# Reordering the loads of a planned attention and expert kernel: first v loads after the first q cast, batch 1 v blocks between casts, batch 2 loads after batch 1 v, dearer v loads in the planner's model

## The chip, the cores and the metric

The kernel runs on one core of one Trainium2 chip. The metric is the device time of one execution in microseconds; lower is better. The kernel before took 360.42 us (median of three, 358.01 to 360.87). A profiled execution has a "span" from its first to its last instruction, some 2 us less than its device time. Each execution has a state: "slow" where it is over 1.5% above the fastest of the same kernel. A median is over all timed executions of a kernel, slow ones too.

## The reference

Windowed attention over 8 batches of 8 heads, 576 positions of 64 values, with a window of 32 on each side; then two matrix products with an ELU between them.

```python
scores = scale * np.matmul(q, k.transpose(0, 1, 3, 2))       # q, k, v: (8, 8, 576, 64)
scores = np.where(np.abs(pos[:, None] - pos[None, :]) <= 32, scores, -1e9)
attn = softmax(scores)
x = np.matmul(attn, v)  -> (4608, 512)
h = x @ w_in                                                  # (512, 2048)
g = np.where(h > 0, h, np.exp(np.minimum(h, 0)) - 1)
return g @ w_out                                              # (2048, 512), float32
```

## The kernel before

All work is cut into named operations, and a planner decides in which order each engine's stream gets them. It simulates engines and DMA queues with estimated durations, and emits in the order of its simulated starts. **Its dependencies become no semaphores.** The waits in the built program come from the data alone, so editing the planner's edges or durations changes the order and nothing else.

```python
class Plan:
    def op(self, name, eng, dur, rank, deps, fn, dma=0.0, wt=1.0, lat=2.0, solo=1.0, soft=()):
        ...
    def run(self):
        ...        # simulated engines and DMA rings; the best ready operation of each engine starts
        for _, n in order:
            ops[n][4]()                      # emit the instructions in that order
```

The names used below: L is a load of half a batch's q or k (issued by ScalarE), C its cast to bf16 (GpSimd from batch 1 on), T its transposes (TensorE) and E their copies out. LV is a load of v (issued by GpSimd), X(i) the transpose of the attention output of pair i (a DMA transpose issued by SyncE from pair 4 on). H is a block of the first product, EX and FF its ELU, Y the second product. Tiles 0 and 1 have two pairs each, the other eight have four.

```python
    def cast(b, nm, half, eng):              # (cut) dst is bf16, src the loaded fp32, 96 x 1536
        if eng is nc.scalar:
            nc.scalar.copy(dst, src)
        else:
            eng.tensor_copy(dst, src)
    ...
    def MK(i):                               # VectorE: both inputs lie in SBUF
        ...
            nc.vector.tensor_mul(dst, pu[:, :, s], mb)
    def FF(t, fo):
        ...
            nc.vector.tensor_scalar(f, e, -1.0, 0.0, ALU.add, ALU.min)
```

The loads of a batch in the plan:

```python
        early = [("H", max(t0 - 2, 0), 2 if b == 2 else 8)] if b > 1 else []
        for half in range(2):
            for nm in ("q", "k"):
                deps = list(early)
                if b == 1:
                    deps.append(("SM", L1AT))
                if b:
                    deps.append(("C", b - 1, nm, half))
                P.op(("L", b, nm, half), "ACT" if b or nm == "q" else "SP", 0.45, ...)
                ...
                P.op(("C", b, nm, half), eng, cdur[eng], need - 30 + half, deps, ...)
        deps = list(early)
        ...
        for qb in range(0, NQB, 2):
            P.op(("LV", b, qb), "POOL", 0.9, ..., deps, ...,
                 dma=1.1 if 0 < qb < NQB - 1 else 0.85, wt=0.02,
                 soft=ring(("LV", b, qb)))
        ...
                P.op(("T", b, nm, hp), "PE", 0.3, need - 36 + 4 * n, deps, ...)
```

The softmax here doesn't subtract the row's maximum and nothing guards it: scores larger than these inputs give would overflow.

## Time and profile before

| | before |
|---|---|
| device time, median of 3 | 360.42 us |
| profiled span | 355.8 us |
| busy: TensorE, VectorE, ScalarE, GpSimd | 88%, 67%, 57%, 24% |
| first exponential of tiles 0, 1, 2, 3, 4 at | 28.9, 44.6, 84.6, 112.1, 147.8 us |

How to read it: TensorE has the most work, so every microsecond in which it waits before its work runs out is lost. The start of each tile's first exponential (ScalarE's first operation on that tile) is a milestone that two kernels can be compared by. The windows of the kernel before show where TensorE's idle time lies. Columns: window, its length, then the busy us of TensorE, weight loads, VectorE, ScalarE and GpSimd with instruction counts, TensorE's clock, DMA share and GB/s.

```profile
0.00:28.90 28.90, 12.74 (x209) 10.67 (x210) 17.92 (x49) 11.67 (x14) 18.09 (x37) 1.00 1.35 201
28.90:44.60 15.70, 12.38 (x116) 9.54 (x115) 13.11 (x29) 11.04 (x29) 7.91 (x8) 1.00 1.30 242
44.60:84.60 40.00, 29.74 (x409) 19.88 (x413) 20.94 (x65) 24.01 (x47) 12.94 (x13) 0.91 1.57 153
84.60:112.10 27.50, 22.64 (x196) 11.54 (x199) 22.43 (x50) 15.69 (x28) 6.03 (x5) 1.00 0.61 116
112.10:147.80 35.70, 32.79 (x319) 17.30 (x323) 27.38 (x54) 23.95 (x39) 14.47 (x14) 1.00 1.10 165
```

Length less TensorE's busy time is its idle time: 16.16, 3.32, 10.26, 4.86 and 2.91 us. The third window, from tile 1's start to tile 2's, also runs at a mean clock of 0.91. The batch 2 loads are issued here, in ScalarE's timeline (columns: start, duration, engine, line, operation):

```profile
45.93 0.32 ACTq L217 DMA_DIRECT2D stg<-in_k_dram  x1
...
47.89 0.43 ACTq L217 DMA_DIRECT2D stg<-in_q_dram  x1
```

### The profile page before, as it was taken

Reading aid. Unit: us, or ns where it says so; the run is one execution under the profiler, and the core shown is the slowest. Engines: PE = TensorE matmul, PEld = TensorE weight load, DVE = VectorE, ACT = ScalarE, POOL = GpSimd, SP = SyncE. Lnnn points to the kernel's source line nnn. Section 1 sums busy time; section 2 is a strip of 40 time slices with the busy share of each in tenths; the row PEclk is TensorE's granted clock in tenths of the full one; section 3 lists DMA queues with packets and bytes.
Section 4 is the critical chain, followed back from the end, with each engine's and each line's share of the span. In section 5 each row is a group of like instructions: output and inputs, shape, how many; then the busy total and the mean of one; then the engine's idle time right before and its main releaser. Section 6 shows DMA issues by size and latency. Waiting matters only on the chain.

```text
span 355.8 us, 7172 instructions
## 1 busy us (share of the span) xinstructions
PE 311.7 (88%) x2788; PEld 170.0 (48%) x2832; DVE 237.0 (67%) x526; ACT 202.5 (57%) x347; POOL 85.3 (24%) x96
## 2 busy tenths in 40 slices
PE   0568782998977988999999999999999999999995
PEld 0456551664433534544454455445544544444442
DVE  5567853576896589767976777689667767665500
ACT  2446772765656755765666666667564655544421
POOL 8643633700037037001620370033000000000000
PEclk9999997899999999999999999999999999999999
DMA  7999999793299999916793889294411211110021
GB/s 195 189 204 271 219 137 248 69 137 99 62 229 140 85 241 153 148 44 173 185 161 58 228 150 150 49 265 118 98 53 46 59 46 44 46 60 29 31 85 63
DMA packets 80561, 45.08 MB, mean 127 GB/s; under 512 B 56336, under 2 KB 76048, under 8 KB 80528
## 3 DMA queue, kind: packets, MB, share of 16 engines
q0 software_dynamic: 41728, 8.92, 33.2%
q1 hardware_dynamic: 26656, 17.88, 22.6%
q10 hardware_dynamic: 12144, 17.83, 20.7%
q8 instruction: 22, 0.36, 0.4%
q14 instruction: 11, 0.09, 0.1%
HBM read 36.70 MB, written 9.44 MB: 130 GB/s over the span
## 4 chain that ended last, share of the span: by engine, by line
PE 62%; DMA 19%; DVE 12%; issue 2%; ACT 2%; ACTq 1%; POOL 0%; POOLq 0%; DVEq 0%
PE psH L381 26%; PE psY L424 25%; DMA stg<-in_q_dram 7%; DMA vw<-in_v_dram 7%; DMA xt<-xs 5%; DVE f L401 3%; PE psT L242 3%; PE psO L334 3%; DVE pm L322 2%; DVE g L410 2%; PE psS L301 2%; DVE xs L349 2%; ACTq L217 1%; ACT e L389 1%; PE psO L424 1%
## 5 line engine op out<-in xcount | busy, mean ns | idle before, releaser
L381 PE MATMUL psH<-xt,w_in_sb 128*128 128x512 bf16 (+1 forms) x623 | 146.7, 360 | 10.8 <-DVE g L410 5.8
L389 ACT ACTIVATE e<-psH 128x512 f32<-128x512 f32 (+1 forms) x160 | 87.8, 555 | 95.0 <-PE psH L381 86.9
L424 PE MATMUL psY<-w_out_sb,g 128*128 128x512 bf16 x501 | 129.1, 380 | 2.1 <-issue 0.9
L381 PEld LDWEIGHTS <-w_in_sb 128*128 128x128 bf16 x640 | 60.2, 99 | 67.7 <-issue 10.0
L401 DVE TENSOR_SCALAR f<-e 128x512 bf16<-128x512 f32 (+1 forms) x112 | 57.9, 517 | 32.3 <-ACT e L389 31.9
L424 PEld LDWEIGHTS <-g 128*128 128x128 bf16 x576 | 52.6, 98 | 54.6 <-issue 0.9
L232 POOL CAST bf<-stg 96x1536 bf16<-96x1536 f32 x28 | 41.1, 1469 | 143.4 <-DMA stg<-in_k_dram 120.8
L410 DVE TENSOR_TENSOR g<-psH,f 128x512 bf16<-128x512 f32 (+1 forms) x112 | 73.1, 652 | 3.5
L407 DVE SCALAR_TENSOR_TENSOR g<-f,psH 128x512 bf16<-128x512 bf16 (+1 forms) x48 | 28.5, 594 | 21.6 <-ACT f L399 21.4
L242 PE MATMUL psT<-ident,bf 96*128 96x96 bf16 x348 | 25.1, 210 | 19.5 <-DVE bf L232 12.5
L309 ACT ACTIVATE pu<-psS 128x1024 bf16<-128x1024 f32 x36 | 36.8, 1024 | 7.7 <-PE psS L301 6.6
L242 PEld LDWEIGHTS <-bf 96*128 96x128 bf16 x384 | 23.8, 104 | 28.8 <-DVE bf L232 12.7
L265 POOL DMA_DIRECT2D vw<-in_v_dram x40 | 34.6, 877 | 12.1 <-DMA w_in_sb<-in_moe_w_in_dram 5.7
L322 DVE TENSOR_TENSOR pm<-pu,masks 128x512 bf16<-128x512 bf16 x72 | 31.9, 485 | 6.0 <-ACT pu L309 5.9
L334 PEld LDWEIGHTS <-pm 128*128 128x128 bf16 x576 | 26.4, 101 | 15.5 <-DVE xs L349 5.4
L334 PE MATMUL psO<-vw,pm 128*128 128x65 bf16 x544 | 29.4, 196 | 4.7 <-DVE xs L349 3.5
L349 DVE TENSOR_TENSOR xs<-psO,rc 128x256 bf16<-128x256 f32 x68 | 28.9, 424 | 4.0 <-DMA xt<-xs 1.7
L347 DVE RECIPROCAL rc<-psO 128x4 f32<-128x4 f32 x68 | 12.2, 179 | 26.3 <-PE psO L334 26.1
L255 ACT COPY qT<-psT 128x576 bf16<-128x576 bf16 x30 | 19.0, 634 | 15.5 <-PE psT L242 15.3
L399 ACT ACTIVATE f<-e 128x512 bf16<-128x512 f32 (+1 forms) x48 | 26.9, 560 | 1.3
L434 ACT COPY y<-psY 128x512 f32<-128x512 f32 x33 | 19.0, 576 | 8.3 <-remote 5.7
L255 ACT COPY kT<-psT 128x576 bf16<-128x576 bf16 x28 | 17.8, 637 | 4.9 <-PE psT L242 4.9
(45 smaller groups left out, 88.1 us busy)
## 6 DMA issues: line engine op xcount, KB each, us to landing
stg<-in_q_dram ACTq DMA_DIRECT2D x16, 576.0 KB, 10.9
out_dram<-y SPq DMA_DIRECT2D x35, 256.0 KB, 2.2
stg<-in_k_dram ACTq DMA_DIRECT2D x14, 576.0 KB, 9.0
vw<-vw SPq DMA_DIRECT2D x12, 260.0 KB, 6.1
vw<-in_v_dram POOLq DMA_DIRECT2D x24, 128.0 KB, 6.3
w_in_sb<-in_moe_w_in_dram POOLq DMA_DIRECT2D x4, 512.0 KB, 12.0
w_out_sb<-in_moe_w_out_dram POOLq DMA_DIRECT2D x4, 512.0 KB, 23.2
vw<-in_v_dram POOLq DMA_DIRECT2D x16, 96.0 KB, 7.0
```

What stands on the lines that cost most here:

```text
L232: eng.tensor_copy(dst, src)
L242: nc.tensor.transpose(pt[:, j, :], src[:, j, 2 * hp:2 * hp + 2, :], ident[0:PR, 0:PR])
L255: nc.scalar.copy(dst, src)
L309: nc.scalar.activation(pu, live.pop(("S", i)), AX.Exp, scale=SCALE)
L322: nc.vector.tensor_mul(dst, pu[:, :, s], mb)
L334: nc.tensor.matmul(o[:, j, :], lhsT=p[:, h, s * QB:s * QB + 128], rhs=vw[b % NVB][:, qb, h, :], start=(s == 0), stop=(s == 1))
L349: nc.vector.tensor_mul(live["X", i][:, g * HP:(g + 1) * HP, :], o[:, :, 0:D], rb)
L381: nc.tensor.matmul(ps, lhsT=w_in_sb[:, do, fo * 128:(fo + 1) * 128], rhs=xts[t][:, do, :], start=(do == 0), stop=(do == NDO - 1))
L389: nc.scalar.activation(e, ps, AX.Exp)
L401: nc.vector.tensor_scalar(f, e, -1.0, 0.0, ALU.add, ALU.min)
L410: nc.vector.tensor_tensor(gs[t][:, fo, :], ps, f, ALU.max)
L424: nc.tensor.matmul(ps, lhsT=gs[t][:, fo, c * 128:(c + 1) * 128], rhs=w_out_sb[:, fo, :], start=(fo == 0), stop=(fo == NFO - 1))
```

## The change

The intent: keep the first v loads out of the way of the first q and k, let batch 1's casts go before the v blocks that are not urgent, and hold batch 2's loads until batch 1's v blocks are through, so that they don't fall into that backlog. The planner's durations for v loads are raised as well.

```diff
+    AHEAD = {(1, 4): [("C", 1, "k", 0)], (1, 6): [("C", 1, "q", 0)],
+             (1, 8): [("C", 1, "k", 1)]}
...
                 if b == 1:
                     deps.append(("SM", L1AT))
+                if b == 2:
+                    deps.append(("LV", 1, 8))
...
+        if b == 0:
+            deps.append(("C", 0, "q", 0))
...
             P.op(("LV", b, qb), "POOL", 0.9,
                  RING.index(("LV", b, qb)) - 999 if b < 2 else r0 + 0.1 * qb,
-                 deps, lambda b=b, qb=qb: load_v(b, qb),
-                 dma=1.1 if 0 < qb < NQB - 1 else 0.85, wt=0.02,
+                 deps + AHEAD.get((b, qb), []), lambda b=b, qb=qb: load_v(b, qb),
+                 dma=1.5 if 0 < qb < NQB - 1 else 1.2, wt=0.04,
+                 solo=1.4,
                  soft=ring(("LV", b, qb)))
```

## The prediction

> **What bounds the kernel now.** I read the page's first two parts, then the windows, then the timelines around the longest hole in TensorE, then each transfer's issue and landing.
>
> ```profile
> span 355.8 us, 7172 instructions
> PE 311.7 (88%) x2788; PEld 170.0 (48%) x2832; DVE 237.0 (67%) x526; ACT 202.5 (57%) x347; POOL 85.3 (24%) x96
> ...
> PE   0568782998977988999999999999999999999995
> ...
> PEclk9999997899999999999999999999999999999999
> DMA  7999999793299999916793889294411211110021
> ```
>
> TensorE is the bound from slice 17 (about 146 us) to the end (nines throughout). All that can be won are its holes before that, 44 us in sum: the start, one deep hole in slice 7 (the digit 2) where the granted clock also falls, and small ones in slices 12 to 16. The DMA engines are full for the first 62 us. The hole, as the windows (busy us of each engine, then clock, DMA share, GB/s) and the TensorE timeline show it:
>
> ```profile
> 55.50:61.80 6.30, 0.01 (x1) 0.01 (x1) 1.58 (x6) 0.38 (x1) 2.93 (x2) 0.74 1.24 263
> 61.80:65.50 3.70, 3.48 (x38) 2.17 (x40) 0.00 (x0) 2.24 (x4) 1.46 (x1) 0.52 0.93 125
> ```
>
> ```profile
> 54.45 1.04 PE L381 MATMUL psH<-xt,w_in_sb 128*128 128x256 bf16 x8
> 61.80 0.66 PE L242 MATMUL psT<-ident,bf 96*128 96x96 bf16 x6 [6.31 <-POOL bf L232]
> 62.39 0.75 PE L301 MATMUL psS<-qT,kT 64*64 64x64 bf16 x24
> ```
>
> TensorE stands 6.31 us before the first transpose of batch 2, which waits for GpSimd's cast of batch 2's q, and then runs 3.7 us at half clock. The chain of waits says why the cast was late:
>
> ```profile
> 46.95 13.18 DMA stg<-in_q_dram
> 60.13 0.02 issue
> 60.15 0.04 POOLq L232
> 60.19 0.08 issue
> 60.27 1.48 POOL bf L232
> ```
>
> The load took 13.2 us because it was issued into the v queue's backlog. Batch 4's loads, issued at 123.57 to 125.04 with little beside them, landed 5.1, 7.6, 10.1 and 12.5 us after the first issue. And the hole is of order, not of work: TensorE's stream in the built program has that transpose before the scores of pair 5, while twelve blocks of the first layer and Y products, which need nothing of batch 2, stand behind it.
>
> **What the Trainium skill says.** "PSUM — Partial Sum Buffer", section "Engine vs sequencer instructions": matmuls start and complete in program order; the hole agrees (nothing overtakes the transpose for 6.31 us). "TensorE: Matmul & The Clock Gate", section "Part 1: The HAM clock gate": after an idle window of about 3.4 us the array runs at half clock until it has been busy as long; the trace agrees (0.52 for 3.7 us after the hole). "DMA: Bandwidth & Descriptors", section "Queues, rings and completion order": each DMA engine takes the queues in turn, a packet at a time. The trace agrees: in 52 to 60 us the q/k queue moved 1.54 MB in 1036 packets and the v queue, in 256 B packets of source, only 0.13 MB in 1009. "SBUF — State Buffer", section "Who interferes with whom": a GpSimd operation and a VectorE cast or scalar operation that both want the shared port exclude each other; the trace agrees (an f of 0.42 us took 1.57 us at 100.68, beside a cast).
>
> **The change part by part.** The diff edits a planner that only writes the order of each engine's stream. I compared the waits of the two built programs: the edges become no semaphores unless the data already need them.
> - *First v loads after the first q cast.* Nothing on the chip: GpSimd's first v load waits for VectorE's third count (the memsets) in both programs and stands in the same place. It was issued at 5.19 us and will be again. As a side effect the planner moves batch 0's last k transposes and their copies ahead of two v shifts. Before, those copies ran at 16.27 and 17.69 us; now the second can start at about 16.75. Gain: 17.69 - 16.75 = **0.95 us** at the start.
> - *Batch 1 v blocks between the casts.* The last three batch 1 v loads move on GpSimd from before the four casts to between them. In the trace those loads were issued at 24.47, 28.03, 32.90 but landed at 49.59, 51.28 and 52.12, because they stand in one queue behind the weights, the last of which landed at 47.48. Issued at 32 to 39 us they still stand behind it: no landing moves. The first cast need no longer wait until 33.68 (its data landed at 31.49), but the q cast waits for its data (35.51) in both. About **0**.
> - *Batch 2 loads after batch 1 v.* No wait, but on ScalarE the four issues move from after block 1 of tile 1 to after block 11, and TensorE's stream has all sixteen blocks of tile 1, the scores of pairs 5 to 8 and six of eight Y products ahead of batch 2's first transpose. That transpose takes its place behind 14 us of work. Gain: 6.31 us of hole, and the slow clock after it: 0.66 + 0.75 + 1.04 us for groups that take 0.42, 0.54 and 0.60 warm, and 1.33 for three Y products that take some 0.81, together 3.78 - 2.37 = 1.4. **7.7 us** in all.
> - *Dearer v loads in the planner's model* move later batches' work by a few places. Between the issue of batch 3's loads and tile 3's first block TensorE has about 3.5 us more work than before (its pure work of that stretch, counted by product at 0.86, score 0.35, AV 0.28 and transpose 0.26 us, goes from 10.9 to 14.4). In the trace that stretch ended in a wait for a transpose of X issued at 105.05 and landed at 110.94, just after the last batch 3 load (110.42); TensorE was busy 2.35 of 5 us in 107 to 112. Part of the 2.65 us fills: **1.2 us**.
>
> Will batch 2's data come in time? Tile 1's block 9 ended at 55.49. With the earlier start, three Y products taken from before it, and ScalarE's stop for issuing at 45.93 to 48.33 gone, I put it at 53 us; two blocks, a Y product and a score later ScalarE issues the loads, at 56.3. The v queue should be empty by about 57, so q lands at 56.3 + 7.6 = 63.9 and is cast by 65.4. TensorE reaches the transpose after 8 Y, 7 AV, 3 scores and 4 blocks, about 69: 3 to 4 us to spare.
>
> New costs: transposes of X that fall among q/k loads land only when these have drained (issued 97.52, landed 110.44). Pairs 4 to 6 now fall there (drained at about 69), and pair 7's, issued at about 72 with batch 3's v loads, must land before tile 2 starts: **1.5 us** of waiting. Batch 2's casts now meet a busy VectorE instead of a stopped one: four collisions of 1.15 us, of which I charge **1 us**.
>
> Sum: 0.95 + 7.7 + 1.2 - 1.5 - 1.0 = 7.35 us. From 146 us on TensorE is busy 97% in both orders, so what is won before is kept. 360.4 - 7.4 = **353.0 us**.
>
> **The rivals.**
> 1. *The hole moves.* The loads go out some 10 us later. If they drain at 72 instead of 69, the transpose waits again, or VectorE's normalisation of pair 7 does, whose buffer is freed only by pair 4's transpose of X. For it: these loads took 17.8 us to land before. Against: that was beside the v backlog. It would cost 3 to 6 us, so 356 to 359.
> 2. *Everything fits.* No new waits, and the batch 3 wait vanishes whole: 0.95 + 7.7 + 2.65 = 11.3 us, so 349.
> 3. *Nothing gained:* the DMA engines bound the first 62 us and only the place of waiting changes. Against: the hole ends with the loads that TensorE need not have waited for, and DMA had empty slices (1 and 2 in tenths at 89 to 98 us). About 360.
> 4. *VectorE becomes the bound* of the stretch after 55 us: 11.5 us of work there and casts beside it. It would take 2 us of the gain.
>
> **Range and chances.** Two per cent is 7.2 us, almost the central gain, so faster and same are near even. Executions of the kernel before spread from 358.01 to 360.87, small beside the doubt in the new waits. Eight in ten: 348.5 to 358.8. Slower would need a hole as large as the one removed and more: 0.03.
>
> **What would show it.** Right: the first v load still issued at about 5.2; last k copy at 16.7; no hole of over 2 us between 50 and 66 and clock 1.0 there; batch 2 loads issued at 55 to 58 and landed within 13 us; tile 2's first 512-wide block at about 77 us instead of 83.55, tile 3's at about 104 instead of 110.9; the rest parallel to before. Wrong: a hole of 3 us or more before the batch 2 transposes, or VectorE waiting on X's landing near 70; or the same spans after tile 3 stretched.

## The result, and the profile after

The change is correct. Its median is 353.9 us (349.42 to 358.22, four executions), against 359.41 us (358.01 to 360.87, four) for the kernel before. The ratio is 0.9724, with a 95% interval of 0.9654 to 0.9794: faster. A ratio is the mean time of one kernel's fast executions over that of the other's in the same rounds, so it is not quite the ratio of the medians. Here it is 349.51 (of 350.67, 349.42 and 348.43 us) over 359.43.

The change's first profiled execution fell in the slow state (358.22 us), and so did one timed execution (357.13). I ran the same kernel again, got a fast profiled execution (350.02 us), and read that one. Everything called "after" below is that profile. Its page:

```profile
span 348.0 us, 7219 instructions
...
PE 315.5 (91%) x2832; PEld 169.8 (49%) x2832; DVE 237.3 (68%) x526; ACT 203.1 (58%) x347; POOL 84.9 (24%) x96
...
PE   0579799989686999999999999999999999999995
...
PEclk9999999999989999999999999999999999999999
```

The 2 of slice 7 is gone, and so is the slow clock there. There is a new shallow place in slices 11 and 13 (6 and 6), with one clock digit of 8 between them, at about 87 to 113 us. The windows of the old hole and TensorE's timeline after it:

```profile
55.50:61.80 6.30, 6.30 (x121) 4.22 (x120) 5.02 (x18) 4.10 (x8) 1.46 (x1) 1.00 1.10 256
61.80:65.50 3.70, 3.70 (x35) 2.07 (x33) 3.54 (x11) 1.79 (x4) 1.96 (x2) 1.00 1.13 241
```

```profile
65.61 0.41 PE L334 MATMUL psO<-vw,pm 128*128 128x65 bf16 x8
65.86 0.42 PE L242 MATMUL psT<-ident,bf 96*128 96x96 bf16 x6
...
73.58 1.90 PE L381 MATMUL psH<-xt,w_in_sb 128*128 128x512 bf16 x8 [0.26 <-DMA xt<-xs]
...
107.89 1.02 PE L381 MATMUL psH<-xt,w_in_sb 128*128 128x512 bf16 x4 [2.64 <-issue]
```

TensorE is busy for all 10 us, at full clock, and takes batch 2's first transpose at 65.86 without a wait. Tile 2's first 512-wide block starts at 73.58, tile 3's at 107.89 after an idle 2.64 us (square brackets: idle time and what ended it). The profile calls that wait "issue". I read it as a wait for the transpose of pair 11, which landed at 107.80 us; that is an inference from the times. The windows by milestone:

```profile
0.00:28.20 28.20, 12.57 (x206) 10.56 (x207) 17.87 (x49) 11.89 (x14) 16.39 (x35) 1.00 1.37 199
28.20:44.00 15.80, 12.86 (x119) 9.70 (x118) 10.81 (x27) 11.71 (x30) 9.13 (x9) 1.00 1.29 246
44.00:74.70 30.70, 28.96 (x372) 18.54 (x370) 21.66 (x63) 20.31 (x44) 13.25 (x13) 1.00 2.03 175
74.70:109.00 34.30, 26.82 (x262) 13.82 (x261) 26.05 (x52) 20.40 (x34) 9.98 (x9) 0.95 1.06 141
109.00:139.90 30.90, 30.77 (x300) 16.11 (x297) 24.68 (x52) 21.60 (x36) 9.08 (x8) 1.00 0.65 130
```

| stretch, to the start of | length before, after | idle before, after | gained in all by its end |
|---|---|---|---|
| tile 0 | 28.9, 28.2 | 16.16, 15.63 | 0.7 |
| tile 1 | 15.7, 15.8 | 3.32, 2.94 | 0.6 |
| tile 2 | 40.0, 30.7 | 10.26, 1.74 | 9.9 |
| tile 3 | 27.5, 34.3 | 4.86, 7.48 | 3.1 |
| tile 4 | 35.7, 30.9 | 2.91, 0.13 | 7.9 |
| the end | 208.0, 208.1 | | 7.8 |

So 9.3 us are won before tile 2, 6.8 are given back before tile 3, 4.8 come back before tile 4, and from there the two run in parallel. (44 matmul records are missing from the trace before: at most four in a stretch before tile 4, of at most 0.22 us each. Its idle times may be too long by up to 0.9 us.)

**What holds tile 3 up.** Its pair 11 was transposed late. SyncE's timeline gives the issue; the DMA view of that moment gives the median time from issue to landing of what was issued in it:

```profile
101.22 1.19 SPq L360 DMA_TRANSPOSE xt<-xs  x1
```

```profile
vw<-in_v_dram POOLq DMA_DIRECT2D x1, 128.0 KB, 5.8
xt<-xs SPq DMA_TRANSPOSE x1, 6.6
```

Batch 4's five v loads were issued from 98.94 on and the transpose took 6.6 us beside them. VectorE, which feeds that transpose, shows why it came only at 101.22:

```profile
89.87 1.10 DVE L401 TENSOR_SCALAR f<-e 128x512 bf16<-128x512 f32 x1
...
92.15 1.09 DVE L401 TENSOR_SCALAR f<-e 128x512 bf16<-128x512 f32 x1
...
93.89 2.00 DVE L322 TENSOR_TENSOR pm<-pu,masks 128x512 bf16<-128x512 bf16 x2
...
97.89 1.39 DVE L401 TENSOR_SCALAR f<-e 128x512 bf16<-128x512 f32 x1
```

An f takes 0.42 us when it is alone (88.26 us) and the pair of mask products 0.75 (102.37). GpSimd's four casts of batch 3 ran at these very times, the first of them here:

```profile
89.22 1.46 POOL L232 CAST bf<-stg 96x1536 bf16<-96x1536 f32 x1 [16.30 <-DMA stg<-in_k_dram]
...
98.94 4.18 POOL L265 DMA_DIRECT2D vw<-in_v_dram  x5
```

The first f ends at 90.97 us, 0.29 after the cast's end at 90.68: it stood until the cast was over. The excess is 0.68 + 0.67 + 1.25 + 0.97 = 3.6 us, on the chain from FF to H (an H block needs the g of three blocks before it, which needs that block's f) and to pair 11's normalisation. TensorE's short waits for these g, and the half clock from 96.4 to 99.8 us that comes after them, also lie before pair 11's last attention product, which runs at 100.10 us.

### The profile page after: what moved, and what is told of

It reads as the page before. It is cut to its first block, busy times and chain, and to the rows that moved or that the text cites. A ratio compares the mean times of both kernels' runs of the same rounds, so it can differ in the third digit from the quotient of the medians.

```text
span 356.2 us, 7175 instructions
## 1 busy us (share of the span) xinstructions
PE 317.2 (89%) x2788; PEld 171.3 (48%) x2832; DVE 239.4 (67%) x526; ACT 203.5 (57%) x347; POOL 85.6 (24%) x96
## 4 chain that ended last, share of the span: by engine, by line
PE 68%; DVE 15%; DMA 10%; issue 3%; ACT 2%; ACTq 1%; POOL 0%
PE psH L381 29%; PE psY L424 26%; DMA stg<-in_q_dram 7%; DVE f L401 4%; PE psO L334 4%; DVE g L410 4%; PE psT L242 4%; DMA xt<-xs 3%; DVE pm L322 3%; PE psS L301 2%; DVE xs L349 2%; PE psO L424 1%; PE psS L424 1%; PE psT L424 1%; ACTq L217 1%
## 5 line engine op out<-in xcount | busy, mean ns | idle before, releaser
L381 PE MATMUL psH<-xt,w_in_sb 128*128 128x512 bf16 (+1 forms) x623 | 152.1, 370 | 10.9 <-DMA xt<-xs 3.9
L381 PEld LDWEIGHTS <-w_in_sb 128*128 128x128 bf16 x640 | 61.4, 101 | 67.5 <-issue 13.4
L401 DVE TENSOR_SCALAR f<-e 128x512 bf16<-128x512 f32 (+1 forms) x112 | 58.8, 525 | 36.5 <-ACT e L389 36.5
L232 POOL CAST bf<-stg 96x1536 bf16<-96x1536 f32 x28 | 41.9, 1498 | 151.9 <-DMA stg<-in_k_dram 124.4
L242 PE MATMUL psT<-ident,bf 96*128 96x96 bf16 x348 | 25.9, 213 | 15.3 <-DVE bf L232 12.4
L322 DVE TENSOR_TENSOR pm<-pu,masks 128x512 bf16<-128x512 bf16 x72 | 34.1, 516 | 1.4 <-ACT pu L309 1.2
L349 DVE TENSOR_TENSOR xs<-psO,rc 128x256 bf16<-128x256 f32 x68 | 28.9, 425 | 2.4
```

The costliest lines, as they stand in the source:

```text
L242: nc.tensor.transpose(pt[:, j, :], src[:, j, 2 * hp:2 * hp + 2, :], ident[0:PR, 0:PR])
L349: nc.vector.tensor_mul(live["X", i][:, g * HP:(g + 1) * HP, :], o[:, :, 0:D], rb)
L381: nc.tensor.matmul(ps, lhsT=w_in_sb[:, do, fo * 128:(fo + 1) * 128], rhs=xts[t][:, do, :], start=(do == 0), stop=(do == NDO - 1))
```

## The experiments

**Theory.** (a) What is gained is the place of batch 2's first transposes in TensorE's stream, not a wait of the loads. (b) What is lost again before tile 3 is lost to whole casts that hold VectorE, which makes pair 11's transpose late and puts it behind the v loads. **Rivals.** The loads' later issue on ScalarE is what gains; the first v loads in fact compete with the first q and k; the v loads alone, as DMA traffic, make tile 3 late, whatever VectorE does.

The kernel before ran beside each group: medians of 359.04 us (first call), 358.29 (second) and 359.77 (third), each call on another chip. In the first call one of its eleven executions took 351.30 us. This makes all the others "slow", so no ratio was given there. The change itself did not run in the second and third calls.

### The change again

No edit.

> The changed kernel once more, to get a trace of a fast execution and to count its two times. Theory (clock): executions near 349 and near 357 come from the same program; the fast trace shows the same order and about the same waits for transposes of X, but the granted clock at 1.0 between 66 and 84 us, where the slow trace had 0.66 to 0.75; tile 2's first 512-wide block at about 76 to 78 us and tile 3's at about 104. Rival (transfers): in the fast trace pair 7's transpose of X lands over 2 us sooner after its issue than the 6.6 us of the slow one, and the clock follows from that. Ratio to before 0.970 to 0.978 of the fast runs; at least one execution in five near 357.

Median 351.6 us, of 350.02, 355.05, 357.02, 351.92, 351.29 and 350.58. Of all eleven executions of the change, four took over 355 us. The profile of the fastest of these six is the one read above. Of the expectation, one of the six is near 357 us and the clock is 1.0 from 66 to 84 us. Tile 2's first block came at 73.58 us, sooner than expected, and tile 3's at 107.89, later than 104. Pair 7's transpose landed 4.2 us after its issue, where it took 6.6 us in the slow profile, as the rival said.

### The transposes later, nothing else

On the kernel before, batch 2's first transpose waits in the plan for pair 7's product. The loads stay early, at about 46 us.

```diff
+                if (b, nm, hp) == (2, "q", 0):
+                    deps.append(("AV", 7, 0))
```

> The kernel before with one edge more in the planner: batch 2's first transpose after the AV of pair 7. Batch 2's loads stay where they were in ScalarE's stream (issue at about 46 us). Theory (the order on TensorE is what counts): the 6.3 us hole before batch 2's first transpose is gone and most of the gain is there, 350 to 354 us, ratio 0.972 to 0.985. Rival (the loads had to go out later, clear of the v queue): with the loads still in the v backlog they land at 57 to 66 us as before and v blocks later, something else stands, and the time is 356 to 360, ratio above 0.988.

353.46 us (352.8 to 355.29): 5.6 us below the median before. The profiled execution was the longest of the four. Tile 2's first block in TensorE's timeline:

```profile
78.12 2.32 PE L381 MATMUL psH<-xt,w_in_sb 128*128 128x512 bf16 x5 [3.33 <-DMA xt<-xs]
```

The hole before the transposes is gone without moving a load, which speaks for (a). Instead tile 2 waits 3.33 us for its input, so this version starts tile 2 at 80.0 us where the change starts it at 74.7. So (a) is shown for the hole, and not for all of the gain before tile 2.

### The change without its edge for batch 2's loads

```diff
-                if b == 2:
-                    deps.append(("LV", 1, 8))
```

> The changed kernel without the edge of batch 2's loads on batch 1's v. The planner then issues these loads early again (before block 2 of tile 1) and puts batch 2's first transpose right after block 11 of tile 1. Theory (order): TensorE stands again before that transpose, 3 to 6 us at about 54 to 60 us, and the clock falls there; 355 to 359 us, ratio 0.987 to 0.998. Rival (v edges carry the gain): without a hole of over 2 us and as fast as the whole change, ratio below 0.980.

351.51 us (349.84 to 357.15), as fast as the change. But the hole is there:

```profile
58.24 0.54 PE L242 MATMUL psT<-ident,bf 96*128 96x96 bf16 x6 [3.04 <-POOL bf L232]
```

It waits 3.04 us for the cast, with 3.4 us of half clock after it, and starts tile 2 at 79.8 us instead of 74.7. It then starts tile 3 at 106.4 instead of 109.0 and tile 4 at 140.4, half a microsecond behind. So the edge removes a hole and the slow clock after it, as the prediction said, though 3.04 us of hole and not 6.31: the other parts of the change had removed the rest. Something later takes all of the gain back. The time alone would have said that the edge does nothing.

### That edge alone

```diff
+                if b == 2:
+                    deps.append(("LV", 1, 8))
```

> The kernel before with only the edge of batch 2's loads on batch 1's v. The planner issues the loads after block 7 of tile 1 and puts batch 2's first transpose after block 12, before the scores of pair 7, between the places of before and of the change. Theory (order): the transpose is reached at about 60 us, its cast done at about 62 to 63, so 2 to 3 us of hole remain; 353 to 357 us, ratio 0.980 to 0.992. If the edge alone carries the whole change: below 0.978.

357.74 us (355.15 to 359.58), slightly above what I had expected. The hole is nearly gone:

```profile
63.96 0.43 PE L242 MATMUL psT<-ident,bf 96*128 96x96 bf16 x6 [0.47 <-POOL bf L232]
```

Tile 2 starts at 79.9 us, 4.7 earlier than before, and tile 3 at 106.6, 5.5 earlier. Tile 4 comes at 147.2 us, only 0.6 earlier: TensorE waited 1.85 us at 104.7 and 2.35 us at 145.3 for transposes of X. The edge alone is not enough.

### Only the dearer v loads of the model

```diff
-                 dma=1.1 if 0 < qb < NQB - 1 else 0.85, wt=0.02,
+                 dma=1.5 if 0 < qb < NQB - 1 else 1.2, wt=0.04,
+                 solo=1.4,
```

> The kernel before with only the dearer v loads in the planner's model, none of the three edges. The planner then puts batch 2's first transpose after block 14 of tile 1. Theory (where the planner puts that transpose decides, whatever edge moves it): no hole over 2 us before it, 350 to 354 us, ratio 0.972 to 0.985 although no edge of the change is there. Rival (the edges carry the gain): 356 to 360, ratio above 0.990.

353.61 us (351.44 to 356.28), ratio 0.9852 (0.978 to 0.9924). Its profiled execution was its longest, 356.28 us, and has other waits: 3.26 us at 38.4 for a g of VectorE, and 2.15 us at 84.0 for X. The hole before batch 2's transposes is gone here too: between 53 and 67 us TensorE has no wait of 0.4 us or more. Three numbers that no instruction depends on are worth about as much as the late transposes; they act through the order alone.

### Batch 4's v loads behind the casts

If the v loads alone hold up pair 11's transpose, moving them helps. On the change, each later batch's v loads come after that batch's last q cast in the plan.

```diff
             if b >= NVB:
+                deps.append(("C", b, "q", 1))
```

> The changed kernel with one edge more in the planner: from batch 3 on a batch's v loads after that batch's last cast, so that they no longer go out just ahead of the transpose of X on which the next tile waits. The order up to tile 2 is that of the change. Theory (v loads' shadow): pair 7's transpose of X lands within 4.5 us of its issue in every execution, not 4.2 in the fast and 6.6 in the slow trace, and pair 11's in 4 to 5 us instead of 6.6; the wait before tile 3's first block shrinks from 2.6 to under 1 us, so 346 to 349 in a fast execution, 2 to 4 us under the change's 350 to 352. Rival (batch 3's q/k loads and VectorE set tile 3's start): no change over 1 us.

351.42 us (348.52 to 356.14, that one slow), ratio 0.9761 (0.9685 to 0.9836): no clear gain over the change. Half of what I expected came: pair 7's transpose, issued at 68.12, landed in 2.4 us instead of 4.2. But at tile 3 the v loads of another batch (97.23 to 100.61) now stood before pair 11's transpose, issued at 98.87. The DMA view of that moment:

```profile
xt<-xs SPq DMA_TRANSPOSE x1, 5.9
```

TensorE waited 2.21 us there. Other v loads had taken the place of those that were moved, so this neither refutes the rival nor confirms it.

### The casts in three pieces

The plan, and with it every engine's order, stays that of the change; only each GpSimd cast becomes three.

```diff
+        elif eng is nc.gpsimd:
+            for t0 in range(0, TPP, 2):
+                eng.tensor_copy(dst[:, :, t0:t0 + 2], src[:, :, t0:t0 + 2])
```

> The changed kernel with each GpSimd cast of 1.47 us done as three of a third; the order of everything else is the same. Theory (VectorE waits for a whole cast when it meets one): the f of 0.28 and 0.42 us that took up to 1.6 us beside a cast take at most 1.0; the two stretches where VectorE is full beside casts (about 90 to 100 and 125 to 138 us) shorten by 1 to 2 us each; 347 to 350 us in a fast execution, and the slow ones near 357 become rarer. Rival (casts beside VectorE cost nothing on the path, or three small casts collide as long in sum): within 1 us of the change.

343.66 us (342.46 to 343.78), ratio 0.9564 (0.9513 to 0.9615): faster. The two other versions of the change in the same call, the late v loads and the real wait below, took 351.4 and 351.3, so the pieces are worth some 7.7 us, more than I had expected. The profiles agree: the span falls from 348.0 us (in the first call) to 340.4, and 6.6 of these 7.6 us are won before tile 3 starts (102.3 us instead of 109.0, with 0.4 of it before tile 2). VectorE's timeline in the same stretch:

```profile
89.29 0.42 DVE L404 TENSOR_SCALAR f<-e 128x512 bf16<-128x512 f32 x1
...
90.90 0.42 DVE L404 TENSOR_SCALAR f<-e 128x512 bf16<-128x512 f32 x1
...
91.96 1.41 DVE L325 TENSOR_TENSOR pm<-pu,masks 128x512 bf16<-128x512 bf16 x2
...
93.89 0.60 DVE L404 TENSOR_SCALAR f<-e 128x512 bf16<-128x512 f32 x1
```

The f of 1.10, 1.09 and 1.39 us are now 0.42, 0.42 and 0.60, and the masks pair 1.41 instead of 2.00. One cast costs more on GpSimd, which has time:

```profile
88.82 1.92 POOL L233 CAST bf<-stg 96x512 bf16<-96x512 f32 x3 [15.45 <-DMA stg<-in_k_dram]
```

Pair 11's transpose is issued at 97.27 us instead of 101.22, and by the DMA view it lands in 3.0 us:

```profile
xt<-xs SPq DMA_TRANSPOSE x1, 3.0
```

The stretch between the starts of tiles 2 and 3 and the clock row:

```profile
74.30:102.30 28.00, 24.42 (x255) 13.15 (x259) 23.58 (x52) 20.28 (x33) 10.69 (x16) 1.00 0.97 155
...
PEclk9999999999999999999999999999999999999999
```

It takes 28.0 us instead of 34.3, with 3.58 us idle instead of 7.48 and no slow clock. Before tile 2 the pieces change little (31.1 us against 30.7). This shows (b): without the collisions the transpose goes out 4 us sooner (some 1.7 us of it because there is no slow clock) and meets no v backlog. The v loads still matter, but only to a transpose that is already late. For the 2.64 us wait itself both were needed: had the change's transpose landed 3.0 us after its issue at 101.22, it would have been there at 104.2, before TensorE ran out of other work at 105.25 (an estimate from these two traces).

### The first wait made real

On the change, GpSimd copies one element of the cast q before the first v load, so that the load really waits.

```diff
+    scr = const.tile([1, 1], BF16)
...
+        if (b, qb) == (0, 0):
+            nc.gpsimd.tensor_copy(scr, live["q", 0][0:1, 0, 0, 0:1])
```

> The changed kernel with the wait that the planner's edge names made real: GpSimd copies one element of batch 0's first q cast before its first v load, so the load is issued at about 9.5 us instead of 5.2. Theory: the second halves of q and k land about 1 us sooner (12.2 to 12.6 us instead of 13.5), the first scores follow 1 us sooner; the weights land 1 to 2 us later, hidden; so 0.5 to 1.2 us faster than the change, 349 to 351 in a fast execution. Rival: the delay of v and weights shows at the first AV or in the early Y products and the time rises by 1 to 3 us.

351.25 us (350.83 to 352.8), ratio 0.9792 (0.9727 to 0.9857). GpSimd's timeline shows the wait:

```profile
9.73 0.18 POOL L267 COPY scr<-bf 1x1 bf16<-1x1 bf16 x1 [4.47 <-DVE bf L233]
9.86 2.69 POOL L268 DMA_DIRECT2D vw<-in_v_dram  x3
```

The load is issued at 9.86 us instead of 5.2. My expectation of 0.5 to 1.2 us gained at the start is refuted: two halves of q and k landed at 13.80 and 13.39 us, against 13.82 and 13.42 in the change and 13.58 and 13.22 before, and tile 0 starts at 28.3 us, against 28.2 in the change. The weights land 0.6 to 2.9 us later than in the change, which is hidden. The DMA packets of the two traces say why. In the change the GpSimd queue moves its first packet at 10.84 us, 5.7 us after the first v load's issue; with the wait it does so at 11.48. So the issue moved by 4.7 us, the transfer by only 0.6, and from 9 to 12 us q and k moved 0.61 MB in both. The first v loads do not delay the first q and k in a way that shows.

### What the parts are worth once the casts are in pieces

The same pieces on the kernel before and on the change without its batch 2 edge:

> The kernel before with each GpSimd cast in three parts, nothing of the change. It tells what the change is worth where casts no longer hold up VectorE. Theory (order of the transpose and collisions with casts are two separate costs): the 6.3 us hole before batch 2's first transpose stays, a little earlier, and only the stretches where VectorE is full beside casts shorten: 352 to 356 us, ratio 0.982 to 0.993; the split change (343.7) stays 8 to 12 us ahead. Rival (collisions are the greater part of both): 346 to 350, within 6 us of the split change.

> The changed kernel without the edge of batch 2's loads on batch 1's v, and with the casts in three parts. Without the split this kernel was as fast as the change (350 to 352) although it keeps a hole of 3.0 us and a cold clock after it. Theory (the edge is worth its 3 us hole and 1.5 us of slow clock, but in the change the gain was given back at tile 3's start, where a transpose of X came into the next v loads' shadow, and the split frees both of that): 346 to 349, 3 to 5 us behind the split change. Rival (the edge is worth nothing): 343 to 344.5.

| casts in three pieces, on | us, median (range) | ratio (95%) | wait at the first transpose of batch 2 |
|---|---|---|---|
| before | 354.0 (353.3 to 355.36) | 0.9904 (0.9805 to 1.0002) | 4.82 |
| change without the batch 2 edge | 346.94 (345.75 to 348.96) | 0.9703 (0.9617 to 0.9789) | 1.42 |
| change (second call) | 343.66 (342.46 to 343.78) | 0.9564 (0.9513 to 0.9615) | none |

TensorE's lines for the first two:

```profile
60.41 0.34 PE L245 MATMUL psT<-ident,bf 96*128 96x96 bf16 x2 [4.82 <-POOL bf L233]
```

```profile
57.33 0.26 PE L245 MATMUL psT<-ident,bf 96*128 96x96 bf16 x2 [1.42 <-POOL bf L233]
```

With the collisions out of the way the edge is worth 346.94 - 343.66 = 3.3 us and the whole change 354.0 - 343.66 = 10.3 us. These two differences compare two calls, on two chips. Within the third call the change with pieces ran only with the late v loads as well (342.78 us, below); against that version they are 4.2 and 11.2 us. On the kernel before, the pieces alone have a ratio of 0.9904, some 3.4 us, but the interval reaches 1.0002, so that gain is unclear. On the change it is not.

### Further pieces, and the v loads again

Three pieces together with the late v loads, and six pieces (one per step of the same loop):

```diff
+            for t0 in range(0, TPP, 1):
+                eng.tensor_copy(dst[:, :, t0:t0 + 1], src[:, :, t0:t0 + 1])
```

> The changed kernel with the casts in three parts and with each batch's v loads, from batch 3 on, after that batch's casts. Theory: with the split, pair 11's transpose of X already escapes the v loads (landed 3.1 us after issue), so little is left for the edge: 342 to 344, within 1.5 us of the split change. If v loads still stand in a transpose's way elsewhere: 339 to 342.

> The changed kernel with each GpSimd cast in six parts of about 0.25 us. Theory (a VectorE operation waits for at most one part): the waits shrink from at most 0.5 to 0.3 us each; 342 to 344 us, at most 1 us faster than three parts. Rival (each part has a fixed cost on GpSimd and a new collision): the casts take 2 to 3 us each, batch 2's transposes come later, 344 to 348.

Late v loads with three pieces: 342.78 us (342.55 to 344.03), ratio 0.9588 (0.9512 to 0.9663), within 1.5 us of the pieces alone, as expected. Six pieces: 342.12 us (341.51 to 342.27), ratio 0.9559 (0.9487 to 0.9632). All three versions with pieces lie within 2 us; their ratios' intervals overlap. The version with six pieces has the lowest median, and all its executions lie below every execution of both kernels.

## Why the prediction was right or wrong

- **The time.** 353.0 us was predicted and the median was 353.9. The agreement is partly luck: the median lies between two fast and two slow executions. The fast ones average 349.5, near the number of rival 2 (349), though not by its mechanism, since the wait at tile 3 did not vanish. The profiled spans differ by 7.8 us, against 7.35 predicted, but that sum is right because terms of it were wrong in opposite directions.
- **The edges are order and no waits: right.** The first v load went out at 5.18 us (5.2 predicted), and the real wait gained nothing.
- **Start, 0.95 us: right in kind, a little too large.** The second k copy ran at 17.00 us (16.75 predicted, 17.69 before) and tile 0 started 0.7 us earlier.
- **Batch 1 v blocks, about 0: right.** The last three blocks landed at 49.63, 51.21 and 51.98 us, against 49.59, 51.28 and 52.12. I had not seen that a batch 1 transpose would wait 0.93 us for its cast at 36.36.
- **The hole and the slow clock after it, 7.7 us: right in size, only in part for the reason given.** Both are gone. The prediction gave all of it to the batch 2 edge. Without that edge only 3.04 us of hole and the slow clock came back, and the dearer v loads alone leave no hole either: more than one part of the change moves that transpose. The rows that issue the loads, in ScalarE's timeline:

```profile
53.77 0.32 ACTq L217 DMA_DIRECT2D stg<-in_k_dram  x1
...
55.38 0.43 ACTq L217 DMA_DIRECT2D stg<-in_q_dram  x1
```

  That is 1 to 2.5 us sooner than the 56.3 predicted; the loads were drained 13.5 us after the first issue (13 predicted). The q cast was done at 64.1 us and the transpose came at 65.86, so there was 1.8 us to spare and not 3 to 4. Rival 1 was that close.
- **Pair 7's transpose, 1.5 us of waiting: mis-sized.** Issued at 69.30, it landed at 73.53 and cost 0.26 us.
- **Collisions of casts, 1 us: right mechanism, wrong place and size.** Before tile 2 they can have cost TensorE little, as its whole idle time there is 1.74 us. Batch 3's casts cost 3.6 us of VectorE before tile 3, and the pieces showed that this is the cost that counts.
- **Small waits before tile 2: a term left out.** Idle time there fell by 8.5 us (10.26 to 1.74); the hole was 6.31 of it. The other waits fell from 3.95 to 1.48, the 0.26 aside; up to 0.9 of this may be missing records.
- **"Part of the 2.65 us fills: 1.2 us": the step that failed.** The work did move forward: of the 34.3 us to tile 3, 7.48 are idle and half of 3.4, that is 1.7, is lost to a slow clock. This leaves 25.1 us of work, against 22.6 before: 2.5 more (3.5 predicted). But the wait did not shrink. Idle time rose from 4.86 to 7.48, the wait for the transpose is 2.64 where it was 1.93, and tile 3 starts at 107.89, not at 104. I had treated that wait as a fixed end, given by batch 3's loads, into which work could be filled. In fact the loads were drained at 97.48, and the end came from VectorE being held by casts and from batch 4's v loads.
- **"The rest parallel to before": right only from tile 4.** Between the starts of tiles 3 and 4 another 4.8 us were gained: 2.8 us of idle time, and 2.0 us of work that had been done earlier. This gave back what the failed step lost.
- **Two readings of the page were off.** The 44 us of idle time are TensorE's in the whole span; 37.5 us of them lie before tile 4's start at 147.8. And the DMA digit at 89 to 98 us is 2, with the only 1 before the tail at about 151 to 160 us. Neither enters the sum.

**Left open.** Why the kernel before once took 351.30 us. Why the change has executions of over 355 us beside those of 348 to 352: the twelve executions of the three versions of the change with pieces all lie from 341.51 to 344.03 us, which would fit whole casts as a cause but does not prove it. And why a v load that GpSimd issues at 5.18 us moves no packet until 10.84.

## What to carry to other kernels

When a planner's edges become no waits, read its edits as moves in each engine's program order, and ask of each moved instruction what it waits for and what stands behind it. A hole that goes away early in a kernel is only kept if the next wait isn't set by something else; compare milestones stretch by stretch, because a gain and a loss can cancel in the total (the batch 2 edge looked worthless in the time and was worth 3 to 4 us once the next limit was gone). On the evidence of this kernel, a long GpSimd operation on a shared port should be cut into pieces when the VectorE operations beside it are short and on the critical path.

## What the Trainium skill lacked or had wrong

- "SBUF — State Buffer", section "Who interferes with whom", says that the later of the two engines blocks for the whole instruction, and the trace agrees (f 1.10 us instead of 0.42). It does not draw the consequence to cut the GpSimd operation: three pieces took 1.92 us of GpSimd instead of 1.46 and took the kernel from some 351.3 to 343.66 us. That a mask product with both inputs in SBUF contends too, as the page says, agrees: 2.00 us for the pair instead of 0.75.
- "TensorE: Matmul & The Clock Gate", section "Part 1: The HAM clock gate", ties the half clock to an idle window of about 3.4 us; its section "A second HAM failure mode: psum-queue depth-cycling" also has a kernel whose frequent short idles made the clock swing. The page gives no figure for how much short idle time is enough. Here the clock fell for 3.4 us from 96.4 on though no single wait in the 8 us before it was longer than 1.26 us; TensorE was busy 9.00 of 12.50 us from 83.5 to 96, and 1.45 of the last 3.40. Lines of the timeline after:

```profile
94.02 1.02 PE L381 MATMUL psH<-xt,w_in_sb 128*128 128x512 bf16 x4 [1.26 <-DVE g L410]
...
96.54 1.86 PE L381 MATMUL psH<-xt,w_in_sb 128*128 128x512 bf16 x4
```

  The same four matmuls took 1.02 and then 1.86 us. Short waits were enough, in this trace.
- "DMA: Bandwidth & Descriptors" has no figure for how long a small DMA transpose takes beside queues in use: 2.4 and 3.0 us with little beside it, 4.2 to 6.6 beside v loads.
- The same page, section "Queues, rings and completion order", has each DMA engine take the queues in turn. From that I expected the first q and k to land sooner with the v loads held back; they landed at 13.80 and 13.39 us instead of 13.82 and 13.42. This does not show the page wrong: the v loads' queue moved its first packet only at 10.84 us without the wait and at 11.48 with it.
